# Queries, keys and values of paired token tiles by seven block products, with one half of x in SBUF

## The chip, the cores and the metric

The kernel runs on one core of a Trainium2 chip. Its engines are TensorE (PE, matmuls, with its weight loads shown apart as PEld), VectorE (DVE), ScalarE (ACT), GpSimd (POOL) and SyncE (SP, which here issues all DMA transfers). The metric is the device time of one execution in microseconds. The kernel before took 1124.25 us (median of 3 runs, 1122.22 to 1126.07).

## The reference

All is float32; S = 2048 tokens, D = 576 columns, H = 32 heads of 18 columns, F = 4608.

```python
xn = (x - mean) / sqrt(var + 1e-5)                 # over the 576 columns
q, k, v = split(xn @ wqkv)                         # 32 heads of 18
phi = lambda t: where(t > 0, t + 1, exp(t)) + 1e-6
pq, pk = phi(q), phi(k)
kv = einsum("bhsd,bhse->bhde", pk, v)              # one 18x18 state per head, over all tokens
z = einsum("bhsd->bhd", pk)
o = einsum("bhqd,bhde->bhqe", pq, kv) / (einsum("bhqd,bhd->bhq", pq, z) + 1e-6)
s = o @ wo
g = silu(gelu(xn @ w1 + b1) @ w2 + b2)
out = x + s * g
```

The state needs the keys and values of all tokens before the first query can be attended.

## The kernel before

**Numbers in two parts.** A float32 operand of a product is kept as h + l, two tiles of the faster type float32r: ACT copies the value into h (which rounds it), DVE or POOL subtracts h from the value to give l. A product is then hh + hl + lh, three matmuls for each 128 rows of the contraction. The 576 rows are four blocks of 128 and a rest of 64 rows; in the fifth block the upper 64 partitions hold the rest's l part, so it needs two matmuls. One tile's projection to 576 columns is 14 stationaries by two halves of 288 columns, 28 matmuls (`project`).

**Key/value stage.** It goes over 16 tiles of 128 tokens. For each: statistics and norm of x (`layernorm` on DVE with a power on POOL, `normalize_x` on ACT), five PE transposes into PSUM (`transpose_x`), h and l of the transposed x out of PSUM into `xh` and `xl`; 28 matmuls into `pk`; the feature map out of PSUM (`phi`, L226 to L229: exponential on ACT, two operations on DVE); 28 matmuls into `pv`, copied by ACT; ten small matmuls that add the tile to the state (`state`); POOL adds the keys to `zacc` (L441). Beside this, 27 operands for the feed-forward part's W2 are prepared: a sum on POOL (L288), h on ACT (L296), l on DVE (L301), and a store. All 16 tiles of x stay in SBUF as h and l, four blocks of 512 tokens.

**Query stage.** For each tile: 28 matmuls for the query, the feature map, the division by the denominator (POOL, DVE, POOL), five transposes, 28 matmuls with the folded state and Wo, and a store. Before the second tile Wo is folded into the state (`fold_wo`). Beside this, `XSums` makes four sums of blocks of x (s1 to s4) and one of the rests for each half of the tokens, from h and l in turns, 1024 columns at a time on DVE (L337), and splits them (L340, L341); one half is stored for later.

**Feed-forward part.** It goes over 18 steps, nine for each half of the tokens. Its products already use a seven-product scheme: two block rows, two block columns and two halves of the contraction, seven block products in the order 1, 6, 7, 5, 2, 3, 4 (`Up`, matmuls at L819), with DVE adding the results in that order. After the first nine steps the other half's x and sums are loaded from DRAM (L1115).

**Order.** Within the first two stages `in_order` fixes every engine, SP too, to the order in which the code is written. In the feed-forward part tables of step numbers set it. PSUM has three pairs of banks (`bank2`), used in turn by everything that takes a pair, and two single banks (`bank1`), which the state holds in the key/value stage.

## Time and profile before

| what | value |
|---|---|
| median of the runs | 1124.25 us |
| runs | 1122.22, 1124.25, 1126.07 us |
| span of the profiled execution | 1122.4 us |
| mean granted PE clock | 0.995 |
| DMA | 246.71 MB, 220 GB/s in the mean |
| HBM | 151.62 MB read, 92.47 MB written |

The profiled execution has no time of its own beside its span; its span lies 1.85 us below the median of the runs. Rows of groups read: line, engine, operation, output and inputs with shapes, count, busy us, mean ns of one, then the engine's idle time just before them and what ended it. Rows of windows read: from and to, length, busy us (and instructions) of PE, weight loads, DVE, ACT and POOL, the granted clock, the busy share of the DMA engines, GB/s. Rows of a timeline or of the chain read: start, us, engine, line, operation. Records of PE and DVE that follow each other overlap a little, so a mean is a latency and a pace is read from starts.

### The profile page before, as it was taken

Reading aid. Unit: us, or ns where it says so; the run is one execution under the profiler, and the core shown is the slowest. Engines: PE = TensorE matmul, PEld = TensorE weight load, DVE = VectorE, ACT = ScalarE, POOL = GpSimd, SP = SyncE. Lnnn points to the kernel's source line nnn. Section 1 sums busy time; section 2 is a strip of 40 time slices with the busy share of each in tenths; the row PEclk is TensorE's granted clock in tenths of the full one; section 3 lists DMA queues with packets and bytes.
Section 4 is the critical chain, followed back from the end, with each engine's and each line's share of the span. In section 5 each row is a group of like instructions: output and inputs, shape, how many; then the busy total and the mean of one; then the engine's idle time right before and its main releaser. Section 6 shows DMA issues by size and latency. Waiting matters only on the chain.

```text
span 1122.4 us, 18619 instructions
## 1 busy us (share of the span) xinstructions
PE 1108.1 (99%) x7008; PEld 1026.8 (91%) x7008; DVE 811.9 (72%) x1185; ACT 456.8 (41%) x801; POOL 443.0 (39%) x368
## 2 busy tenths in 40 slices
PE   8999998999999999999999999999999999999997
PEld 8999988999998989989889899898898998989987
DVE  6666658787687888878879888666475674764766
ACT  4444443233544454543544544524233242242352
POOL 4556533333353552535525434324233232242340
PEclk9999998999999999999999999999999999999999
DMA  7588631044659468475594769977766666756252
GB/s 295 193 335 301 222 124 41 33 172 160 228 224 342 170 241 301 160 290 206 205 340 172 262 244 389 368 254 258 221 208 212 214 204 211 231 197 222 84 170 88
DMA packets 83367, 246.71 MB, mean 220 GB/s; under 512 B 9229, under 2 KB 19981, under 8 KB 79695
## 3 DMA queue, kind: packets, MB, share of 16 engines
q1 hardware_dynamic: 83279, 245.54, 61.9%
q8 instruction: 55, 0.90, 0.3%
q14 instruction: 33, 0.27, 0.1%
HBM read 151.62 MB, written 92.47 MB: 217 GB/s over the span
## 4 chain that ended last, share of the span: by engine, by line
PE 95%; DVE 3%; DMA 0%; POOL 0%; ACT 0%; issue 0%; SPq 0%; DVEq 0%; ACTq 0%; POOLq 0%
PE pm L950 34%; PE e L819 12%; PE a L819 10%; PE zy L819 10%; PE pv L219 5%; PE pk L219 5%; PE b L819 4%; PE ps_s L592 4%; PE pq L219 4%; PE pd L1074 2%; PE ps_kva L256 1%; PE pt L196 1%; DVE xt L337 1%; PE ps_kw L518 1%; PE ptp L574 0%; DMA w<-wqkv 0%
## 5 line engine op out<-in xcount | busy, mean ns | idle before, releaser
L957 DVE TENSOR_TENSOR macc<-pm,macc 128x576 f32<-128x576 f32 x218 | 164.2, 753 | 56.9 <-PE pm L950 56.3
L616 ACT CAST h_h<-g 128x512 fp32r<-128x512 f32 x204 | 120.9, 621 | 139.8 <-PE pm L950 138.7
L619 DVE TENSOR_TENSOR h_l<-g,h_h 128x512 fp32r<-128x512 f32 x204 | 172.3, 844 | 0.0
L918 POOL TENSOR_TENSOR mid<-g 128x512 f32<-128x512 f32 x34 | 44.1, 1296 | 187.7 <-ACT g L827 187.7
L827 ACT ACTIVATE g<-b,b1c 128x512 f32<-128x512 f32 x36 | 24.8, 688 | 121.8 <-DVE b L845 121.7
L836 ACT COPY mid<-a 128x512 f32<-128x512 f32 x36 | 21.1, 585 | 109.3 <-PE a L819 109.3
L819 PE MATMUL a<-h0r,wa 128*128 128x512 f32 x180 | 58.6, 390 | 0.0
L819 PE MATMUL a<-xh,wa 128*128 128x512 f32 x180 | 58.5, 390 | 0.0
L839 DVE TENSOR_TENSOR mid<-b,mid 128x512 f32<-128x512 f32 x36 | 24.8, 689 | 46.5 <-PE b L819 35.4
L915 POOL TENSOR_TENSOR g<-g 128x512 f32<-128x512 f32 x34 | 52.4, 1542 | 13.1 <-DVE h_l L619 11.8
L912 POOL TENSOR_TENSOR g<-g 128x512 f32<-128x512 f32 x34 | 49.5, 1456 | 17.9 <-DVE h_l L619 16.6
L1044 POOL TENSOR_TENSOR fin1l<-fin1h,fin1l 128x288 f32<-128x288 f32 x8 | 6.4, 805 | 121.4 <-DMA fin1l<-s_dram 45.1
L819 PE MATMUL zy<-xh,w 128*128 128x512 f32 x144 | 50.2, 389 | 0.0
L819 PE MATMUL zy<-h1r,w 128*128 128x512 f32 x144 | 50.2, 389 | 0.0
L641 POOL TENSOR_TENSOR w1t<-w1raw 128x256 f32<-128x256 f32 x18 | 17.6, 977 | 81.4 <-DVE w L619 81.4
L909 POOL TENSOR_TENSOR g<-g 128x512 f32<-128x512 f32 x34 | 47.7, 1402 | 2.7
L852 DVE TENSOR_TENSOR e<-e,mid 128x512 f32<-128x512 f32 x36 | 25.1, 697 | 27.1 <-PE e L819 27.0
L555 POOL TENSOR_TENSOR pbuf<-phiq,den 128x576 f32<-128x576 f32 x16 | 20.9, 1305 | 57.8 <-DVE den L554 52.9
L827 ACT ACTIVATE g<-e,b1c 128x512 f32<-128x512 f32 x36 | 24.8, 689 | 43.0 <-DVE e L852 43.0
L288 POOL TENSOR_TENSOR w2r<-w2r 128x576 f32<-128x576 f32 x27 | 41.1, 1528 | 0.7
L819 PEld LDWEIGHTS a<-xh,wa 128*128 128x128 f32 x180 | 33.8, 188 | 6.8
L819 PEld LDWEIGHTS a<-h0r,wa 128*128 128x128 f32 x180 | 33.8, 188 | 6.8
(814 smaller groups left out, 3544.8 us busy)
## 6 DMA issues: line engine op xcount, KB each, us to landing
op<-w SPq DMA_DIRECT2D x72, 256.0 KB
w<-op SPq DMA_DIRECT2D x72, 256.0 KB
op<-w2o SPq DMA_DIRECT2D x27, 576.0 KB
w2raw<-w SPq DMA_DIRECT2D x10, 1152.0 KB
w1raw<-w SPq DMA_DIRECT2D x18, 640.0 KB
op_a<-wa SPq DMA_DIRECT2D x18, 640.0 KB
wa<-op_a SPq DMA_DIRECT2D x18, 640.0 KB
w2r<-w SPq DMA_DIRECT2D x9, 1152.0 KB
```

The costliest lines, as they stand in the source:

```text
L219: nc.tensor.matmul(ps[:, h, :HD], st, w[:, k, h * HD : (h + 1) * HD], start=(i == 0), stop=(i == len(seq) - 1),)
L592: nc.tensor.matmul(ps[:, h, :HD], st[:, k, :], w[:, k, h * HD : (h + 1) * HD], start=(i == 0), stop=(i == len(seq) - 1),)
L616: nc.scalar.copy(pair[0], src)
L619: eng.tensor_tensor(pair[1], src, pair[0].bitcast(F32), op=SUB)
L819: nc.tensor.matmul(ps, st, mv, start=first and n == 0, stop=n == len(seq) - 1, skip_group_check=True,)
L827: nc.scalar.activation(g, ps, AF.Gelu_apprx_tanh, bias=b1c[:, f : f + 1])
L909: tt(src[5, pr], A(1, 0), A(1, 1), op=ADD)
L912: tt(src[6, pr], src[5, pr], A(0, 0), op=SUB)
L915: tt(src[3, pr], A(0, 1), src[6, pr], op=SUB)
L918: tt(src[7, pr], A(0, 0), A(1, 0), op=SUB)
L950: nc.tensor.matmul(ps[:, q, :HD], hs[p][st][:, cs], m[:, p, :], start=(n == 0 and i not in CHAIN), stop=(n == len(seq) - 1), skip_group_ch ...
L957: nc.vector.tensor_tensor(dst, src, dst, op=ADD)
```

## The change

The seven-product scheme of the feed-forward part is applied to the projections. Two token tiles, one from each quarter of a half's tokens, form a pair (`pair_tile`), and there are eight pairs. `Proj` does both tiles' projection to 576 columns: seven products of six matmuls, four of which also take two matmuls of the rest, 50 in all. DVE makes five additions out of PSUM per pair and projection, ACT two copies. Pair 0's keys and values still go by the plain `project`, 28 matmuls a tile, since the sums aren't there yet.

For that, the weights are kept with their sums (`Weight`: seven h and seven l operands of 2 x 288 columns, and the rest); one tile, `wkq`, holds Wk and later Wq. The sums of x are made in the key/value stage from each pair's transposes: ACT copies the transposed tile to float32 in SBUF (`xf`), POOL makes the five sums (`x_sum`), ACT and DVE split them (`s_hi`, `s_lo`), and x's own split (`x_hi`, `x_lo`) now reads SBUF. `XSums` is gone from the query stage. The feature map also works in SBUF, on the finished keys (`phi_exp`, `phi_max`).

Only one half of x and its sums stays in SBUF (`xH`, `xL`, `xSH`, `xSL`). Each pair is stored to DRAM (`x_store`). The pairs 0 to 3 (second half of the tokens) come first, the pairs 4 to 7 overwrite their columns; the queries start with pairs 4 to 7 and pairs 0 to 3 are loaded back one by one (`x_reload`). After nine feed-forward steps the other half is loaded with four transfers (`x_swap`). A table of steps, 14 to a pair, says after which product each piece of this work is issued (`plan_pair`). W2's sums stand there too, three to a pair for pairs 2 to 6, and the other twelve in the query stage.

On DVE, one tile of the key/value stage reads so before (`xl` and `xh` splits, two W2 splits, statistics, feature map):

```order
L205 TENSOR_TENSOR xl_89<-pt_541,xh_88 128x4x128
L206 TENSOR_TENSOR xh_88<-pt_541,xh_88 64x128
L301 TENSOR_TENSOR w2o_550<-w2r_304,w2o_550 128x576
L301 TENSOR_TENSOR w2o_552<-w2r_306,w2o_552 128x576
L168 BN_STATS st_556<-x_405 128x6
L169 BN_STATS st_556<-x_405 128x6
L171 BN_AGGR mv_559<-st_556 128x2
L172 TENSOR_SCALAR mv_559<-mv_559 128x1
L180 SCALAR_TENSOR_TENSOR mv_559<-mv_559 128x1
L227 TENSOR_SCALAR ek_565<-ek_565 128x576
L229 SCALAR_TENSOR_TENSOR phik_568<-pk_512,ek_565 128x576
```

And now, on DVE, from the feature map of pair 2's keys through the first products of its values (`ab` and `ze` are PSUM, `mu` the running sums, `scr` the float32 copies of x and s):

```order
L387 TENSOR_SCALAR e_151<-e_151 128x576
L388 SCALAR_TENSOR_TENSOR k_147<-k_147,e_151 128x576
L343 TENSOR_TENSOR mu_143<-ab_807,mu_142 128x288
L387 TENSOR_SCALAR e_152<-e_152 128x576
L388 SCALAR_TENSOR_TENSOR k_148<-k_148,e_152 128x576
L346 TENSOR_TENSOR mu_144<-ze_808,mu_143 128x288
L349 TENSOR_TENSOR v_150<-ze_808,mu_144 128x288
L295 TENSOR_TENSOR xSL<-scr,xSH 128x8x128
L299 TENSOR_TENSOR xSH<-scr,xSH 64x128
L355 TENSOR_TENSOR v_149<-ze_808,mu_143 128x288
```

The additions that free PSUM (L343 to L355) stand between the feature map and x's and s's splits, and those read SBUF alone.

On POOL, two tiles read so before (power, W2 sums, sum of the keys):

```order
L173 TENSOR_TENSOR mv_454<-mv_454,nhalf 128x1
L288 TENSOR_TENSOR w2r_304<-w2r_304 128x2x288
L288 TENSOR_TENSOR w2r_306<-w2r_306 128x2x288
L441 TENSOR_TENSOR zacc<-zacc,phik_463 128x576
L173 TENSOR_TENSOR mv_559<-mv_559,nhalf 128x1
L288 TENSOR_TENSOR w2r_306<-w2r_306 128x2x288 x2
L441 TENSOR_TENSOR zacc<-zacc,phik_568 128x576
```

And now, on POOL, one pair, which has five sums of x more:

```order
L235 TENSOR_TENSOR mv_915<-mv_915,nhalf 128x1
L436 TENSOR_TENSOR w2r_687<-w2r_687 128x2x288 x2
L288 TENSOR_TENSOR scr<-scr 128x256 x4
L288 TENSOR_TENSOR scr<-scr 128x128
L235 TENSOR_TENSOR mv_1013<-mv_1013,nhalf 128x1
L436 TENSOR_TENSOR w2r_687<-w2r_687 128x2x288
L554 TENSOR_TENSOR zacc<-zacc,k_147 128x576
L554 TENSOR_TENSOR zacc<-zacc,k_148 128x576
```

One W2 sum less and five sums of x more stand in the same span of tokens.

On ACT, the opening reads so before, from the V weight's casts to the third tile (`pt` is a transposed tile in PSUM, `pk` keys in PSUM):

```order
L243 CAST wv_h<-raw_v 128x576 x4
L243 CAST wv_h<-raw_v_143 128x576
L204 CAST xh_86<-pt_246 128x5x128
L226 ACTIVATE ek_264<-pk_207 128x576
L434 COPY v_298<-pv_269 128x576
L191 ACTIVATE xn_262<-x_193,mv_258 128x576
```

And now, on ACT (`pp` is a plain projection in PSUM, `xn_269` the third tile's norm, `e_151` the exponential of the first tile's keys):

```order
L471 COPY rt<-pt_246 128x640
L479 CAST xSH<-pt_246 128x2x128
L266 CAST xH<-rt 128x3x128
L146 CAST wv_h<-raw_195 128x2x288 x2
L248 ACTIVATE xn_269<-x_202,mv_265 128x576
L248 ACTIVATE xn_269<-x_202,mv_265 128x64
L391 ACTIVATE e_151<-pp_217 128x576
L146 CAST wv_h<-raw_195 128x2x288 x2
L157 CAST wv_rh<-rr_196 128x576
L518 COPY scr<-pt_311 128x640
L264 CAST xH<-scr 128x5x128
```

The first exponential of keys moved behind the third tile's norm, and three of the V weight's casts behind it.

The diff, cut to what the prediction speaks of:

```diff
+    xH = xp.tile([P, 8, 512], F32R, tag="xH", name="xH")
+    xL = xp.tile([P, 6, 512], F32R, tag="xL", name="xL")
+    xSH = xp.tile([P, 9, 512], F32R, tag="xSH", name="xSH")
+    xSL = xp.tile([P, 8, 512], F32R, tag="xSL", name="xSL")
...
+    def x_lo(p, s, src=None):
+        cs, src = pair_cols(p), xf(p, s) if src is None else src
+        tt = nc.vector.tensor_tensor
+        if s == 0:
+            tt(xL[:, 0:4, cs], src[:, :4], xH[:, 0:4, cs].bitcast(F32), op=SUB)
+        else:
+            tt(xL[:, 4:6, cs], src[:, 2:4], xH[:, 5:7, cs].bitcast(F32), op=SUB)
+        r = xH[64:, 4 + 3 * s, cs]
+        tt(r, src[64:, 4], r.bitcast(F32), op=SUB)
...
+    def x_sum(p, i, eng):
+        a, b = xf(p, 0), xf(p, 1)
+        s1, s2, s3, s4 = (s_raw[:, k : k + 2] for k in (0, 2, 4, 6))
+        out, u, v, op = {
+            1: (s1, b[:, 0:2], b[:, 2:4], ADD), 2: (s2, s1, a[:, 0:2], SUB),
+            3: (s3, a[:, 0:2], b[:, 0:2], SUB), 4: (s4, a[:, 2:4], s2, SUB),
+            5: (s_raw[:, 8], a[:, 4], b[:, 4], SUB),
+        }[i]
+        eng.tensor_tensor(out, u, v, op=op)
+    def s_lo(p):
+        cs = pair_cols(p)
         nc.vector.tensor_tensor(
+            xSL[:, :, cs], s_raw[:, :8], xSH[:, :8, cs].bitcast(F32), op=SUB
         )
...
+    def x_store(p):
+        cs = pair_cols(p)
+        for t, a, b in X_PARTS:
+            nc.sync.dma_start(x_dram[p // 4][:, a:b, cs], t[:, :, cs].bitcast(F32))
...
+        def step(self, i):
+            A, B, Z, E = self.A, self.B, self.Z, self.E
+            tt = nc.vector.tensor_tensor
+            a, b = self.dst
+            if i == 1:
+                self.mm(A, 1)
+                nc.scalar.copy(self.m1, A)
+            elif i == 6:
+                self.mm(B, 6)
+                tt(self.u1, B, self.m1, op=ADD)
+            elif i == 7:
+                self.mm(Z, 7)
+                tt(self.u2, Z, self.u1, op=ADD)
+            elif i == 5:
+                self.mm(E, 5, (1, 1))
+                tt(b[:, HD:], E, self.u2, op=ADD)
+            elif i == 2:
+                self.mm(A, 2, (0, 0), first=False)
+                nc.scalar.copy(a[:, :HD], A)
+            elif i == 3:
+                self.mm(E, 3, (1, 2), first=False)
+                tt(a[:, HD:], E, self.u1, op=ADD)
+            else:
+                self.mm(Z, 4, (0, 1))
+                tt(b[:, :HD], Z, self.u2, op=ADD)
...
+    def phi_max(r, e):
+        nc.vector.tensor_scalar(e, e, 1.0, 1e-6, op0=ALU.min, op1=ADD)
+        nc.vector.scalar_tensor_tensor(r, r, 1.000001, e, op0=ADD, op1=ALU.max)
...
+        if 1 <= p and p + 1 < NPAIR and p + 1 >= 2:
+            q = p + 1
+            add(base + 2, transpose_to_xf, q, 1)
+            add(base + 3, x_hi, q, 1)
+            add(base + 4, x_lo, q, 1)
+            for i, at in {1: 3, 2: 3, 3: 4, 4: 4, 5: 5}.items():
+                add(base + at, x_sum, q, i, GP)
+            add(base + 8, s_hi, q)
+            add(base + 10, s_lo, q)
+            add(base + 11, x_store, q)
...
-                for k, at in {"h0": 13, "l0": 13, "s2": 13, "h1": 15, "l1": 15, "s1": 15, "s4": 15}.items():
-                    add(base + at, load_x_part, k)
+                for k, at in ((0, 13), (1, 13), (2, 15), (3, 15)):
+                    add(base + at, x_swap, k)
```

822 lines of the change are left out of this document (426 added, 396 removed), and 4 rows, old and new, of the table SUMS.

## The prediction

> **What bounds the kernel now.** I read the page first: busy times and the shares of the chain of waits.
>
> ```profile
> PE 1108.1 (99%) x7008; PEld 1026.8 (91%) x7008; DVE 811.9 (72%) x1185; ACT 456.8 (41%) x801; POOL 443.0 (39%) x368
> ...
> PE 95%; DVE 3%; DMA 0%; POOL 0%; ACT 0%; issue 0%; SPq 0%; DVEq 0%; ACTq 0%; POOLq 0%
> ```
>
> TensorE (PE) is busy for the whole span and is 95% of the chain, so at first sight fewer matmuls mean less time. Next the windows by stage: busy us and instructions of PE, weight loads, DVE, ACT and POOL, the granted clock, the DMA share.
>
> ```profile
> 13.60:153.00 139.40, 139.32 (x1091) 139.02 (x1090) 92.58 (x166) 62.84 (x104) 75.74 (x67) 1.00 0.68 254
> 153.00:298.20 145.20, 141.05 (x1016) 136.01 (x1015) 110.33 (x163) 52.57 (x99) 49.96 (x39) 0.96 0.32 112
> 298.20:1122.40 824.20, 818.21 (x4849) 743.19 (x4847) 600.64 (x838) 333.35 (x587) 309.89 (x249) 1.00 0.66 231
> ```
>
> The first window is the key/value stage, the second the query/attention stage, the third the feed-forward part, which the change hardly touches. In the first, DVE works 92.58 of 139.40 us and POOL 75.74; in the second PE is idle at least 145.20 - 141.05 = 4.15 us. The chain in order of time gives PE's pieces:
>
> ```profile
> 26.81 3.74 PE pk L219 x28
> 30.55 0.55 PE pt L196 x5
> 31.09 0.88 PE ps_kva L256 x8
> 31.97 0.13 PE ps_kvb L256 x2
> ...
> 321.17 22.43 PE pm L950 x168
> ```
>
> A projection of one tile is 28 matmuls in 3.74 to 3.77 us; the five transposes take 0.55, the state sums 0.88 + 0.13. A token tile costs 3.77 + 3.74 + 0.55 + 1.01 = 9.07 us, a pair 18.1. The last row has 288-column matmuls with a new stationary each time, as the changed projections have: 22.43 / 168 = 0.1335 us.
>
> **What the change takes away on PE.** A pair's projection goes from 56 to 50 matmuls, and 22 of 24 pair-projections change: 132 matmuls, 132 x 0.1335 = 17.6 us. That would be the gain if PE stayed the bound. A pair of the key/value stage would take 100 x 0.1335 + 2 x 0.55 + 2 x 1.01 = 16.5 us instead of 18.1.
>
> **What it puts on DVE and POOL there.** The rows that price this, first of the key/value stage, then of the next:
>
> ```profile
> L180 DVE SCALAR_TENSOR_TENSOR mv<-mv 128x1 f32<-128x1 f32 x13 | 17.9, 1375 | 9.4 <-POOL mv L173 9.4
> L229 DVE SCALAR_TENSOR_TENSOR phik<-pk,ek 128x576 f32<-128x576 f32 x14 | 10.6, 758 | 0.5
> L205 DVE TENSOR_TENSOR xl<-pt,xh 128x512 fp32r<-128x512 f32 x14 | 9.7, 691 | 31.3 <-ACT xh L204 31.3
> L227 DVE TENSOR_SCALAR ek<-ek 128x576 f32<-128x576 f32 x14 | 6.3, 447 | 0.0
> L168 DVE BATCH_NORM_STATS2 st<-x 128x6 f32<-128x288 f32 x13 | 5.9, 453 | 0.0
> L171 DVE BATCH_NORM_AGGREGATE mv<-st 128x2 f32<-128x12 f32 x13 | 2.7, 209 | 0.4
> L206 DVE TENSOR_TENSOR xh<-pt,xh 64x128 fp32r<-64x128 f32 x14 | 4.1, 294 | 0.2
> ```
>
> ```profile
> L525 DVE TENSOR_TENSOR kw_l<-ps_kw,kw_h 128x288 fp32r<-128x288 f32 x2 | 0.9, 457 | 3.8 <-ACT kw_h L524 3.8
> L244 DVE TENSOR_TENSOR kw_l<-kw,kw_h 128x576 fp32r<-128x576 f32 x1 | 0.7, 695 | 0.0
> L337 DVE TENSOR_TENSOR xt<-xt,xh 128x1024 f32<-128x1024 f32 x2 | 2.4, 1218 | 0.0
> ```
>
> ```profile
> L441 POOL TENSOR_TENSOR zacc<-zacc,phik 128x576 f32<-128x576 f32 x14 | 19.8, 1411 | 2.6 <-DVE phik L229 2.6
> L173 POOL TENSOR_TENSOR mv<-mv,nhalf 128x1 f32<-128x1 f32 x13 | 7.1, 549 | 49.1 <-DVE mv L172 49.1
> ```
>
> A middle pair (2 to 5) has on DVE: ten additions out of PSUM, 10 x 0.457 = 4.6, and the statistics of two tiles, 2 x (2 x 0.453 + 0.21 + a one-column add, taken as 0.2) = 2.6. These 7.2 us read at most one operand from SBUF. The others read two, or run in the fast one-input form of L227: three W2 splits 3 x 0.695, x's splits 0.69 + 0.41 + 1.22 + 3 x 0.29, the feature map 2 x (0.447 + 0.695), two one-column products at 0.2 or less, together 8.0. DVE has 15.2 us in all. POOL has five 576-wide operations at 1.41, four 256-wide sums at 0.73 (row below), one of 128 (estimated 0.5), two powers at 0.55: 11.6.
>
> The 8.0 and the 11.6 exclude each other. L180 works on one column and takes 1375 ns when POOL has just begun a W2 sum, and here, in the feed-forward part, operations with two SBUF inputs lengthen on both engines (mean alone 1296 ns on POOL, 0.67 us on DVE):
>
> ```profile
> L918 POOL TENSOR_TENSOR mid<-g 128x512 f32<-128x512 f32 x34 | 44.1, 1296 | 187.7 <-ACT g L827 187.7
> ```
>
> ```profile
> 325.92 1.62 POOL L912 TENSOR_TENSOR g<-g 128x512 f32<-128x512 f32 x1
> 327.62 1.62 POOL L915 TENSOR_TENSOR g<-g 128x512 f32<-128x512 f32 x1
> 331.63 0.73 POOL L646 TENSOR_TENSOR w1raw<-w1raw 128x256 f32<-128x256 f32 x1
> ```
>
> ```profile
> 326.98 1.11 DVE L619 TENSOR_TENSOR h_l<-g,h_h 128x512 fp32r<-128x512 f32 x1
> 328.68 1.11 DVE L619 TENSOR_TENSOR h_l<-g,h_h 128x512 fp32r<-128x512 f32 x1
> 335.43 0.67 DVE L619 TENSOR_TENSOR h_l<-g,h_h 128x512 fp32r<-128x512 f32 x1
> 341.12 0.41 DVE L619 TENSOR_TENSOR w<-w1t,w 128x256 fp32r<-128x256 f32 x1
> ```
>
> POOL's ends are 327.62 + 1.62 - 325.92 - 1.62 = 1.70 us apart, each round holding one POOL and one DVE operation. L205, with one input in PSUM, stays at 691 ns in the mean, as long as L619 alone, though POOL is at work in that stage. So a middle pair needs 8.0 + 11.6 = 19.6 us by full records, or 19.6 x 1.70 / (1.30 + 0.67) = 16.9 by that stretch. Between them lie the chains: the feature map is four such operations in a row, among POOL's third W2 sum and first `zacc` sum, and the addition of product 5 of the values is queued behind it on DVE, before PE may write product 3 into the same bank. I take 19.6, since DVE also waits there for products and for ACT. The ends are 16.5 (PE's own) and 23.
>
> The Trainium skill ("SBUF — State Buffer", section "SBUF: two separate sides") says that the pair of ports shared by the two engines is locked for the whole instruction and the loser blocks. By that the 19.6 stands; by the 1.70 us of this trace part of each record overlaps, the four middle pairs would give 4 x 2.7 = 11 us back, and the sum would be 1144 instead of 1155.
>
> ACT's part, four casts and two copies of x and s, two norms, two exponentials, four copies of 288 columns and three W2 casts, is near 11 us of the 19.6, so I cost it at nothing there. So too the stores of x, 2.03 MB a pair: with W2's stores and loads 5.6 MB in 19.6 us, 284 GB/s, where the first window moved 254 at a DMA share of 0.68. If they aren't hidden, the next x tiles, behind them on SP, come late, and DVE's statistics with them. In pair 1 that is so: the first tile of pair 3 loads behind the first store.
>
> Before, two token tiles cost 18.1, so the middle pairs lose 4 x 1.5. Pair 1 also carries the splits of the V weight's sums and a second split of s: DVE 15.2 - 2.1 + 2 x 1.3 + 1.5 = 17.2, of which 10.0 exclude POOL; POOL four 576-wide weight sums in place of three W2 sums, 13.0; 23.0, plus some 4 us that DVE is late at its start: 27 (22 to 30). Pair 6 lacks the loads ahead, 17. Pair 7 rewrites the weight tile to Wq, five splits on ACT and DVE between the feature map and the additions: 19. Pairs 1 to 7: 27 + 78.4 + 36 = 141.4 against 153.0 - 26.8 = 126.2: **+15.2**, with 114 (-12) and 163 (+37) as ends.
>
> **The opening.** Pair 0 is still projected plainly, two tiles for K, then for V, and everything for pair 1 must be ready behind it. Rows:
>
> ```profile
> 12.85 0.77 PE L196 MATMUL pt<-ident,xn 128*128 128x128 f32 x5 [0.61 <-DVE xn L177]
> 19.60 1.20 ACT L191 ACTIVATE xn<-x,mv 128x576 f32<-128x576 f32 x2 [1.46 <-DVE mv L180]
> ```
>
> ```profile
> L226 ACT ACTIVATE ek<-pk 128x576 f32<-128x576 f32 x15 | 9.8, 654 | 1.4 <-issue 1.4
> L204 ACT CAST xh<-pt 128x640 fp32r<-128x640 f32 x13 | 9.0, 692 | 18.3 <-PE pt L196 18.3
> L296 ACT CAST w2o<-w2r 128x576 fp32r<-128x576 f32 x27 | 16.9, 676 | 0.0
> ```
>
> Up to the second tile's normalized x nothing changes (its transposes at 12.85). Then, step by step: transposes to 13.9; ACT copies it, 0.69, and casts K's part for the plain projection, 0.4, so PE begins tile 1 near 15.1 and ends near 19.0. Its next transposes need the third PSUM pair, which holds tile 0's keys until their feature map is made. That is behind, on ACT, a cast (0.5), two weight casts (2 x 0.68) and the third tile's norm (1.20), which waits for DVE's split and statistics (0.7 + 1.3), POOL's split (1.41) and power (0.55): norm ends at 20.3, exponential 0.65, DVE 0.45 + 0.76: 22.1. The fourth tile repeats it: transposes 22.7; ACT has three weight casts left of which the last ends at 22.9; copy and cast to 24.3; splits, statistics, power, norm to 29.0; exponential; one POOL sum to wait for; feature map 31.6; transposes 32.2. Then pair 1's sums: copy and cast 33.5; DVE splits and two sums, with POOL between, 36.0; a weight split of 1152 columns (about 1.3) 37.3; POOL 0.73 + 0.5; ACT's cast of s (about 1.2) 39.8; DVE's split 1.5; the fifth tile's statistics, power, product, 43.2; norm 44.4; transposes 45.0. PE's work in this stretch is four projections and four transposes, and it is idle for the rest. Before, the same point (two tiles projected) stands at 26.81. **+18.2**; without any POOL wait about +13, with one more operation in each round +22.
>
> **Clock.** In the query stage a PE wait of 1.69 us is followed by slower matmuls (below), and that window's granted clock is 0.96 where the key/value stage has 1.00:
>
> ```profile
> 183.52 0.74 PE L574 MATMUL ptp<-ident,pbuf 128*128 128x128 f32 x5 [1.69 <-DVE phiq L229]
> ...
> 185.30 0.64 PE L592 MATMUL ps_s<-kw_h,th 128*128 128x288 f32 x2
> ```
>
> Waits of 2 to 4 us inside each pair could do the same, some 3 us of slow PE each time, mostly hidden while DVE is the bound. I add **+2**, between 0 and 8. The Trainium skill ("TensorE: Matmul & The Clock Gate", "What's actually happening") has the clock halved only after about 3.4 us of idleness; by it the term would be nearly 0, by the row above it can come sooner.
>
> **The query stage.** Eight pairs at 50 instead of 56 matmuls: 48 x 0.1335 = 6.4 less. x's sums, 20 operations of 1024 columns, and their splits leave DVE, so the waits of the second window go down from 4.15 or more; four rounds get W2 splits before the addition that frees product 3's bank. Net 1 better: **-7.5** (-11 to -3). The reloads of x (2 MB a round) stand on SP ahead of Wo's row shifts, and the DMA share of that window is 0.32, so they fit.
>
> **The feed-forward part.** The reload of the other half's x, 31 x 512 x 128 x 4 bytes = 8.1 MB, comes where DMA is full:
>
> ```profile
> L1115 SPq DMA_DIRECT2D l0r<-x_dram x1: 319/319/319, 680.0 to 680.0; - x1
> ```
>
> ```profile
> L1115 SPq DMA_DIRECT2D s4r<-x_dram x1: 320/320/320, 694.4 to 694.4; - x1
> ```
>
> ```profile
> 684.50:708.30 23.80, 23.80 (x176) 23.53 (x175) 19.81 (x28) 9.22 (x14) 7.96 (x6) 1.00 1.01 415
> ```
>
> Before, its first three parts are issued from 680.0, during the last products. Now each of the four tiles is read until product 3 or 4, so all start near 684.5, 4.5 us later, and the sums that landed last must be there for product 6 instead of product 3. At 415 GB/s a full delay is up to 6 us; how much slack there was no row shows: **+2.5** (0 to 6).
>
> **Sum.** 18.2 + 15.2 + 2 - 7.5 + 2.5 = +30.4; span 1122.4 + 30.4 = 1152.8. The profiled span lies 1.85 below the median of the runs, 1124.25, which I keep: **1155 us**. Under 0.3% (3.4 us) a difference can't be told here.
>
> **Rivals.**
> - *PE stays the bound* (0.10): DVE and POOL fit beside 16.5 us per pair. For it: PE is never idle in 27 to 153 us and POOL's records overlap. Against: 15.2 us of DVE work of 16.5. Pairs 114 (-12), query -7.5, reload 0, opening +8: 1124.25 - 11.8 = 1112. It decides the sign if the pairs run at 16.5 and the opening loses under 17.
> - *The exchange is cheaper* (0.22): the 1.70 us rows hold and the chains cost little. Against it: nothing but the orders, in which the same waits come back each pair. Middle pairs 17.3, pair 1 22, the last two 33, opening +14: 14 - 2 - 7.5 + 1 = +5.5, 1130 (1121 to 1140).
> - *Waits and slow clock feed each other* (0.20): for it the 183.52 row, against it that PE has 3 us to spare per pair. PE stops before product 3 of the values, resumes at half pace, DVE then waits for it: middle pairs 23, pair 1 30, last two 41, opening +20: 20 + 36.8 - 4 + 4 = +57, 1181.
> - The change not doing what it says: the instruction order has 132 matmuls fewer, so this is left out.
>
> **Numbers.** My forecast (1140 to 1170) has 0.46; the rest, 0.02, is a stall that I don't see. To hold 8 in 10 the range goes from 1126 to 1182: it leaves out the first rival, the low end of the second and the high end of the third. Faster 0.09, within 0.3% 0.06, slower 0.85.
>
> **What would show it.** The first seven-product matmul at about 45 us; middle pairs 19 to 21 us apart with PE idle before product 3, released by DVE; DVE's L388 and L295 longer than 0.7 and 1.2 us where POOL runs; the first feed-forward matmul near 326 us instead of 298. I am wrong if DVE is idle between products in the middle pairs, or the opening ends before 35.

## The result, and the profile after

The changed kernel took 1256.8 us (median of 4 runs, 1255.4 to 1258.2) against 1124.05 us for the kernel before: a ratio of 1.118, with a 95% interval from 1.117 to 1.120. The forecast was 1155 us, between 1126 and 1182. The direction was right and the size was four times too small.

The profiled span is 1255.0 us. First the page of the changed kernel, engines and the chain that ended last:

```profile
PE 1136.6 (91%) x6876; PEld 1037.4 (83%) x6876; DVE 851.7 (68%) x1283; ACT 480.7 (38%) x850; POOL 494.2 (39%) x419
...
PE 76%; DVE 9%; DMA 7%; ACT 3%; issue 2%; SPq 1%; POOL 1%; DVEq 0%; POOLq 0%; ACTq 0%
```

PE has the 132 matmuls less, and still records 28 us more busy time; in the first two windows below the granted clock is 0.91, so its matmuls take longer there. Its share of the chain fell from 95% to 76%, so it now waits, for DVE, DMA and ACT. Next the windows by stage (busy us of PE, weight loads, DVE, ACT, POOL; granted clock, DMA share, GB/s): pairs 1 to 7, the query stage, the feed-forward part. The first begins with the first seven-product matmul, the second with the first for queries.

```profile
46.38:242.83 196.45, 137.50 (x897) 127.47 (x896) 119.56 (x213) 70.65 (x119) 93.56 (x90) 0.91 0.55 180
242.83:428.85 186.02, 150.96 (x979) 139.88 (x978) 103.58 (x180) 56.81 (x114) 66.51 (x51) 0.91 0.48 161
428.85:1255.00 826.15, 818.59 (x4849) 743.10 (x4847) 601.83 (x838) 333.33 (x587) 310.18 (x249) 1.00 0.66 231
```

No engine fills the first two windows: in the pairs PE is busy for 137.5 of 196.5 us, DVE for 119.6, POOL for 93.6. That is a picture of engines waiting for each other, and not of one that is full. Against the stages of the kernel before:

| stage | before | after | difference | forecast |
|---|---|---|---|---|
| opening, to the first seven-product matmul (before: to the third tile's keys) | 26.8 | 46.4 | +19.6 | +18.2 |
| pairs 1 to 7 | 126.2 | 196.5 | +70.3 | +15.2, and +2 for the clock |
| query stage | 145.2 | 186.0 | +40.8 | -7.5 |
| feed-forward part | 824.2 | 826.2 | +2.0 | +2.5 |
| sum | 1122.4 | 1255.0 | +132.6 | +30.4 |

The middle pairs 2 to 5 are 27.45 us each (82.70 to 192.50 for four), where 19.6 were forecast; pair 1 is 36.3 (forecast 27), pair 6 22.6 (17), pair 7 27.7 (19).

**One middle pair.** The timeline of PE shows where it stands; the last bracket is the idle time before the matmul and what ended it. In time, these are product 6 and product 4 of the keys, product 6 and product 5 of the values:

```profile
139.18 0.40 PE L329 MATMUL ab<-wkq_h,xSH 128*128 128x288 f32 x1 [0.49 <-ACT mu L340]
148.81 0.40 PE L329 MATMUL ze<-wkq_h,xH 128*128 128x288 f32 x1 [1.69 <-DVE k L355]
151.54 0.40 PE L329 MATMUL ab<-wv_h,xSH 128*128 128x288 f32 x1 [0.60 <-ACT mu L340]
157.97 0.61 PE L329 MATMUL ze<-wv_h,xSH 128*128 128x288 f32 x1 [4.57 <-DVE mu L346]
```

None of these four waits is for data, or for a bank that is still read. Product 5 writes bank E, and L346 reads bank Z. Product 4 writes Z, and L355 reads E. Product 6 writes B, and ACT's copy L340 reads A. Each time it is the other bank of the same two-bank PSUM tile. The instruction list of PE, which is the program with its waits before it runs, has these waits too (the last two matmuls of the values' product 7 in a middle pair, then the first two of product 5):

```
L329 MATMUL ze_1236<-wv_l,xSH 128x288
L329 MATMUL ze_1236<-wv_h,xSL 128x288
L329 MATMUL ze_1236<-wv_h,xSH 128x288 [waits DVE_49]
L329 MATMUL ze_1236<-wv_l,xSH 128x288
```

The third row is the first matmul of product 5. Its bank was free, and yet it waits for DVE.

DVE and POOL at the same place in pair 2, the feature map of the second tile's keys on DVE and then L346 (the second fence is POOL):

```profile
99.35 1.28 DVE L387 TENSOR_SCALAR e<-e 128x576 f32<-128x576 f32 x1
100.67 1.83 DVE L388 SCALAR_TENSOR_TENSOR k<-k,e 128x576 f32<-128x576 f32 x1
102.43 0.45 DVE L346 TENSOR_TENSOR mu<-ze,mu 128x288 f32<-128x288 f32 x1
```

```profile
98.65 1.67 POOL L436 TENSOR_TENSOR w2r<-w2r 128x576 f32<-128x576 f32 x1
100.28 1.61 POOL L554 TENSOR_TENSOR zacc<-zacc,k 128x576 f32<-128x576 f32 x1
```

L387 takes 0.45 us and L388 0.76 when POOL is quiet (run e8 below). Here L387 ends at 100.63, 0.31 us after POOL's first sum, and L388 at 102.50, 0.61 us after POOL's second: with the times that they take alone, both did their work when POOL's instruction was all but over. L346 is queued behind them, and PE behind L346.

**One query round.** The chain in order of time, in the second of the four rounds that carry W2 work:

```profile
305.92 8.30 DMA w2r<-w
314.26 0.09 issue
314.35 1.44 POOL w2r L436
315.81 0.68 ACT w2o L440
...
317.79 0.46 DVE rt L349
318.29 2.30 PE ze L329 x8
```

A chunk of W2 lands 8.3 us after its issue, which stands behind the reload of x in SP's list; POOL sums it, ACT casts it, DVE splits it (the row left out), and only then DVE comes to L349, for which product 3 waits. The four rounds take 28.8, 23.8, 24.0 and 20.1 us, the next one without W2 work 18.1.

**The feed-forward part** waits for the second half of x once, as forecast (waits of PE, total, times, longest):

```profile
PE b L954 <- DMA xSL<-x_dram: 1.7, 1, 1.7
```

### The profile page after: what moved, and what is told of

The parts are those of the page before. It is cut to its first block, busy times and chain, and to the rows that moved or that the text cites. A ratio compares the mean times of both kernels' runs of the same rounds, so it can differ in the third digit from the quotient of the medians.

```text
span 1255.0 us, 18591 instructions
## 1 busy us (share of the span) xinstructions
PE 1136.6 (91%) x6876; PEld 1037.4 (83%) x6876; DVE 851.7 (68%) x1283; ACT 480.7 (38%) x850; POOL 494.2 (39%) x419
## 4 chain that ended last, share of the span: by engine, by line
PE 76%; DVE 9%; DMA 7%; ACT 3%; issue 2%; SPq 1%; POOL 1%; DVEq 0%; POOLq 0%; ACTq 0%
PE pm L1085 29%; PE e L954 11%; PE zy L954 9%; PE a L954 9%; PE ze L329 5%; PE b L954 4%; PE ps_s L769 4%; DMA w2r<-w 3%; PE ab L329 2%; DMA xSL<-x_dram 2%; PE pd L1204 2%; ACT xn L248 1%; DVE w2o L445 1%; DMA kr<-kw 1%; DVE e L387 1%
## 5 line engine op out<-in xcount | busy, mean ns | idle before, releaser
L954 PE MATMUL a<-xH,wa 128*128 128x512 f32 x360 | 117.1, 390 | 0.0
L954 PEld LDWEIGHTS a<-xH,wa 128*128 128x128 f32 x360 | 67.6, 188 | 13.6
L962 ACT ACTIVATE g<-b,b1c 128x512 f32<-128x512 f32 x36 | 24.8, 689 | 122.0 <-DVE b L980 122.0
L954 PE MATMUL e<-xSH,wb 128*128 128x512 f32 x216 | 67.6, 394 | 0.0
L974 DVE TENSOR_TENSOR mid<-b,mid 128x512 f32<-128x512 f32 x36 | 24.8, 690 | 47.5 <-PE b L954 36.4
L1047 POOL TENSOR_TENSOR g<-g 128x512 f32<-128x512 f32 x34 | 49.6, 1459 | 18.2 <-DVE h_l L796 16.9
L954 PE MATMUL a<-xL,wa 128*128 128x512 f32 x144 | 56.2, 390 | 0.0
L329 PE MATMUL ze<-wkq_h,xSH 128*128 128x288 f32 x90 | 30.8, 342 | 23.1 <-DVE scr L346 12.1
L954 PEld LDWEIGHTS e<-xSH,wb 128*128 128x128 f32 x216 | 40.5, 188 | 12.1 <-DVE b L980 3.8
L954 PE MATMUL b<-xSH,w 128*128 128x512 f32 x144 | 50.2, 389 | 0.0
L954 PE MATMUL zy<-xSH,w 128*128 128x512 f32 x144 | 50.2, 389 | 0.0
L954 PE MATMUL zy<-xH,w 128*128 128x512 f32 x144 | 50.2, 389 | 0.0
L954 PE MATMUL e<-xSH,w 128*128 128x512 f32 x144 | 50.2, 389 | 0.0
```

The costliest lines, as they stand in the source:

```text
L329: nc.tensor.matmul(ps, st, mv, start=first and n == 0, stop=n == len(seq) - 1, skip_group_check=True,)
L954: nc.tensor.matmul(ps, st, mv, start=first and n == 0, stop=n == len(seq) - 1, skip_group_check=True,)
L1047: tt(src[6, pr], src[5, pr], A(0, 0), op=SUB)
```

## The experiments

All eleven start from the changed kernel; beside them the kernel before took 1123.6 to 1124.7 us. e10 is a median of 4 runs, the others are one run each; the four runs of the changed kernel lie 2.8 us apart, so a difference of 3 us between two runs says nothing by itself. "Pair" is the mean of pairs 2 to 5, from one first matmul of product 1 to the next; "query stage" runs from the first query matmul to the first of the feed-forward part.

| run | edit | time | pair | query stage |
|---|---|---|---|---|
| | changed kernel | 1256.8 | 27.5 | 186.0 |
| e1 | other pairing of PSUM banks | 1215.2 | 23.2 | 172.4 |
| e2 | reloads of x behind the W2 loads | 1242.8 | 27.4 | 173.3 |
| e3 | pairs without W2 work | 1245.3 | 24.7 | 187.8 |
| e4 | PE kept busy in two waits | 1254.0 | 26.3 | 188.0 |
| e5 | e1 and e2 | 1208.8 | 23.3 | 165.4 |
| e6 | e5, lists in another order | 1196.7 | 21.6 | 160.3 |
| e7 | query rounds without W2 work | 1238.1 | 27.4 | 168.6 |
| e8 | e1, POOL quiet in the pairs | 1187.6 | 17.6 | 172.0 |
| e9 | old pairing, POOL quiet in the pairs | 1233.0 | 21.8 | 187.9 |
| e10 | e6, lists ordered further | 1192.4 | 20.7 | 161.8 |
| e11 | e10, query rounds without W2 work | 1182.6 | 20.8 | 151.6 |

### e1: which banks share a tile

```diff
-            self.A, self.B = ab[:, 0, :HD], ab[:, 1, :HD]
-            self.Z, self.E = ze[:, 0, :HD], ze[:, 1, :HD]
...
+            self.A, self.Z = az[:, 0, :HD], az[:, 1, :HD]
+            self.B, self.E = be[:, 0, :HD], be[:, 1, :HD]
```

(The lines left out take the two tiles in alternating order from one projection to the next. The pairing and this order were not tried apart.)

> The edit: the seven products' four PSUM banks are paired as A with Z and B with E, in place of A with B and Z with E, and the order in which the two pairs are taken alternates, so that the tile product 1 needs is the one read earlier. Nothing else changes. In the trace of the changed kernel PE stands before product 5 until DVE's second addition, L346, is done (4.6 us in each middle pair), which reads Z while product 5 writes E; before product 4 until L355, which reads E while product 4 writes Z (1.7 and 0.5 us); before product 6 until ACT's copy of A (0.5 us, 13.8 us over the program). Theory 'a wait holds for the whole PSUM tile': these waits are for the other bank of the same tile, and they go or shrink to what the other pairing leaves. Middle pairs 27.5 down to 21 to 23 us, the 6.3 us before product 6 of pair 1 down to under 1, the late query rounds unchanged near 18: total 1205 to 1220 us. Rival 'DVE's list sets the pace': PE would only wait at another product, since DVE still does the two feature maps of the keys before L346: middle pairs 26 to 27.5, total 1243 to 1255.

Measured: 1215.2 us, pairs of 24.0, 22.5, 22.9 and 23.3, the query stage 13.6 us shorter. In the same 54 us of time the waits of PE were (total, times, longest), first in the changed kernel, then here:

```profile
PE ze L329 <- DVE mu L346: 9.1, 2, 4.6
PE ze L329 <- DVE k L355: 3.4, 2, 1.7
PE ab L329 <- ACT mu L340: 2.2, 4, 0.6
PE ze L329 <- DVE v L355: 1.1, 2, 0.6
```

```profile
PE be L335 <- DVE mu L349: 5.2, 3, 1.9
PE az L335 <- ACT mu L346: 5.2, 3, 1.7
PE az L335 <- DVE mu L352: 0.3, 1, 0.3
```

(The same additions are L343, L346 and so on in the one, six lines further down in the other: L349 is the old L343, which reads B, beside E.) The waits behind the second addition and behind L355 are gone; what is left are the waits that this pairing has, again for the other bank of the tile: product 5, which writes E, waits for L349, which reads B, and product 7, which writes Z, for ACT's L346, which copies A. Not one operation differs, so the wait for the whole tile is shown. What this pairing and order save of it is 41.5 us of span, and some of it is left. Theory "DVE's list sets the pace" falls. The first theory's total holds and its mean pair is 0.2 us over its range; but the 6.3 us in pair 1 became 3.3 us before product 7, where under 1 was expected.

### e2: the reload of x behind the W2 load

```diff
-            if r < NPAIR // 2:
-                x_reload(Q_ORDER[r + 4])
             if 1 <= r <= 4:
                 w2_load(r + 4, w2rp, "w2raw")
...
             if r == 0:
                 fold_wo()
+            if r < NPAIR // 2:
+                x_reload(Q_ORDER[r + 4])
```

> The edit: in the query rounds the four reloads of x stand behind the load of a W2 chunk on SP, and in the first round behind the fold of Wo with its row shifts; the K/V stage is untouched. Theory 'the reload stands in the way': in the changed kernel the chain has 11.0 us for the row shifts kr, issued behind 2 MB of reloads, and three rounds of 24 us with 4.4 us of reload issues on SP and then 8.3 to 8.7 us for a W2 chunk of 1.18 MB. With the chunk first, it starts 4.4 us sooner and has the queues to itself, 4 to 5 us: rounds of 24 become 16 to 18, row shifts 4 to 5; query stage 20 to 30 us shorter, total 1225 to 1235. Rival 'one W2 buffer': the load can't start before the round's last split has read the buffer, and the first sum of the next round needs it, so a round can't be shorter than load plus sum plus cast whatever stands before it: only the 4.4 us of issues go, rounds of 19.5 to 21, total 1240 to 1246.

Measured: 1242.8 us; rounds of 20.1. The W2 load no longer ends the wait; the chain of a round is now

```profile
305.90 1.16 POOL pbuf L733
307.06 1.41 POOL w2r L436
308.49 0.68 ACT w2o L440
...
310.94 1.52 DVE w2o L445
312.88 1.32 PE ze L329 x8
```

So the place of the reload cost 4 us in each of three rounds (the fourth took 20.1 us before), and the rest of the chain, sum, cast and split ahead of the addition, stays. The wait for the row shifts in the first rounds didn't get shorter (11.0 us, then 11.7): it was not made by the reload ahead of them. The rival's ranges for the total and for the rounds hold, but not by its reason: the load, which it put at the head of each round, is no longer on the chain.

### e3: pairs without W2 work

```diff
-                add(base + a, w2_sum, 3 * c + j)
-                add(base + b, w2_hi, 3 * c + j)
-                add(base + d, w2_lo, 3 * c + j)
+                add(base + d, w2_put, 3 * c + j)
```

(`w2_put` stores the raw block in both places of the operand.)

> The edit: in pairs 2 to 6 the three W2 sums on POOL, the casts on ACT and the splits on DVE are left out, and the raw blocks are stored in their place with the same bytes, so the first five chunks of W2 hold raw values and not the operands. What is left out in a pair is POOL 4.5, ACT 2.0 and DVE 2.6 us, and the DVE time that the splits wait (1.8 us before the second, for ACT). Theory 'exclusive port', as predicted: DVE's and POOL's two-input operations can't overlap, so the pairs shorten by the sum of both, 4.5 + 2.6 = 7 us, to 20 or 21: total 1215 to 1222. Theory 'waits of the whole PSUM tile, and the half clock behind them': only the waits on ACT and the lengthened L388 (1.83 for 0.76) go, 3 us a pair, to 24 or 25: total 1237 to 1243.

Measured: 1245.3 us, pairs of 24.7. Taking 4.5 us of POOL and 2.6 us of DVE work from a pair gave 2.8 us. The sum of the two engines' exclusive work does not set the pair; the second theory's range for the pair holds, and the total lies 2 us above its range.

### e4: PE kept busy

```diff
...
+            for _ in range(n):
+                nc.tensor.matmul(
+                    ps_kv[1][:, 128:416], xH[:, 0, self.cs], self.w.op(1)[0][:, 0],
+                    start=False, stop=False, skip_group_check=True,
+                )
```

(n is 32 ahead of the values' product 5 and 12 ahead of the keys' product 4, in pairs 1 to 6.)

> The edit: matmuls of no use (288 columns, into columns of the state's second bank that nothing reads) are put on PE ahead of product 5 of the values (32) and of product 4 of the keys (12) in pairs 1 to 6, so that PE doesn't idle there; 32 at 0.1335 us are 4.3 of the 4.6 us that it waited. The result's values are unchanged. Theory 'half clock': behind each of these waits the next products ran at half pace (eight matmuls in 2.29 us instead of 1.07, five transposes in 1.07 instead of 0.55), and DVE then waited for them (2.4 us before L349): with PE kept busy the pairs lose 1.8 to 2.5 us each, total 1240 to 1244. Rival 'DVE has slack behind the wait': the pairs keep 27 to 27.5 us, total 1251 to 1256.

Measured: 1254.0 us, pairs of 26.3. The values' product 5 starts when the second addition ends (L346, here L357), as in the changed kernel, and runs at full pace:

```profile
126.53 0.38 DVE mu L357
126.95 1.33 PE ze L330 x8
128.28 0.55 PE pt L258 x5
```

Eight matmuls in 1.33 us for 2.29, five transposes in 0.55 for 1.07; but the pair gains only 1.15 us, less than the first theory's 1.8 and more than the rival's 0.5. Most of the pair's length is there without the half pace. The span is 2.7 us shorter, which one run can't tell from nothing: pairs 1 to 5 gained 6.1 us, pair 6 lost 2.0, and the query stage, which the edit leaves alone, came out 2.0 longer. The total lies in the range of the rival "DVE has slack".

### e5: both edits together

The edit is the two diffs of e1 and e2.

> The edit: the new pairing of PSUM banks (A with Z, B with E) and the later reloads of x together. Apart, the first took 41 us from the span (29 in the K/V pairs, 13.6 in the query stage) and the second 14, all in the query stage. If they remove different waits there, they add up: 1255 - 41 - 14, 1199 to 1204 us. If the rounds of 24 us are one chain, from a chunk's landing through sum, cast and split to the addition that frees product 3's or 4's bank, each takes out part of the same chain: 1207 to 1214.

Measured: 1208.8 us. Apart the edits took 41.5 and 13.9 us from the span, together 47.9 (in the query stage 13.6 and 12.7 apart, 20.6 together): in the query rounds they take out parts of the same chain, from the chunk to the addition that product 3 or 4 waits for. The second reading holds.

### e6: the lists in another order

```diff
-        add(base + 8, phi_max, k_t[1], e_t[1])
+        add(base + 9, phi_max, k_t[1], e_t[1])
...
-            for j, (a, b, d) in enumerate(((0, 3, 3), (2, 5, 5), (6, 9, 13))):
+            for j, (a, b, d) in enumerate(((0, 3, 4), (2, 4, 6), (6, 9, 13))):
...
-                    add(base + 2 * j, w2_sum, n)
-                    add(base + 2 * j + 1, w2_hi, n)
-                    add(base + 2 * j + 2, w2_lo, n)
+                    add(base + j, w2_sum, n)
+                    add(base + (2, 4, 5)[j], w2_hi, n)
+                    add(base + (3, 5, 6)[j], w2_lo, n)
```

> The edit: on top of the new bank pairing and the later reloads, the lists are put in another order. K/V pairs: the second feature map of the keys stands behind the addition of product 7 of the values (L346 in the changed kernel) instead of ahead of it; the first two W2 splits on DVE one step later, so that DVE doesn't wait for ACT's cast. Query rounds: each split of W2 behind an addition instead of ahead of it. No operation is added or taken away. Theory 'the lists' order costs, not the engines' capacity': with the same work the middle pairs, 22.8 us with the new pairing, go to 19 to 20.5, the rounds of W2 to 17 to 18: 20 to 28 us less than the run with pairing and reloads alone, 1175 to 1184. Theory 'exclusive port' as predicted: DVE's two-input operations and POOL's need 19.6 us a pair only if they never wait, so the order brings at most 1 us a pair: 5 to 10 us less.

Measured: 1196.7 us, 12.1 us less than e5, pairs of 21.6, W2 rounds of 17.6 to 23.8. That is between the two theories, nearer to the second: the order is worth something, but with all the work in place the pairs don't come to 20.

### e7: query rounds without W2 work

```diff
-                    add(base + 2 * j, w2_sum, n)
-                    add(base + 2 * j + 1, w2_hi, n)
-                    add(base + 2 * j + 2, w2_lo, n)
+                    add(base + 2 * j + 2, w2_put, n)
```

> The edit, against the changed kernel: in the query rounds the W2 chunks are loaded and stored as before, but not summed, cast and split (POOL, ACT, DVE); so four chunks of W2 hold raw values and not the operands. The reloads stand where they were. Theory 'a chain from the load through the W2 work': in the rounds of 24 us product 3 waits for an addition that is queued on DVE behind a split, that for a cast, that for a sum, that for the load. Without this work rounds 2 to 5 take what the later ones take, 18 us: 4 x 6 = 24 us less, total 1228 to 1234. Rival 'the transfers': the reloads and chunks themselves hold the round, 22 us or more: total 1246 to 1252.

Measured: 1238.1 us; the two rounds that took 24 us now take 18.1, with the reloads and loads in their old places:

```profile
303.66:321.72 18.06, 15.90 (x119) 15.20 (x118) 10.20 (x19) 5.04 (x11) 5.31 (x5) 1.00 0.95 307
```

(Window of one round; busy PE, weight loads, DVE, ACT, POOL, clock, DMA share, GB/s.) So the transfers themselves don't hold a round; the chain through sum, cast and split does. The span is 18.6 us shorter where 24 were expected: the round ahead of them went from 28.8 only to 24.8, held by the row shifts, and the one behind them from 20.1 to 18.4.

### e8 and e9: a quiet POOL, with the new pairing and with the old

```diff
-        add(base + 9, k_sum, k_t[0])
-        add(base + 11, k_sum, k_t[1])
```

(and the edit of e3; e8 has that of e1 too)

> The edit: on top of the new bank pairing the W2 sums, casts and splits of pairs 2 to 6 (raw blocks stored instead) and the sums of the keys' feature map on POOL (so the denominator is only 1e-6) are left out. In a middle pair POOL keeps five small sums of x and two powers, 4.6 us instead of 12.7; DVE loses 2.6 us of splits. Theory 'exclusive port': with POOL quiet, L387 and L388 go back from 1.23 and 1.85 us to 0.45 and 0.76, and the middle pairs, 22.8 us with the pairing alone, go to PE's own 16.5 to 17.5: spans 27 to 32 us under that run, 1182 to 1187 total. Theory 'the lists still wait for each other': L388 shortens all the same, but the pairs stay at 19.5 to 21: 1197 to 1205.

> The edit: the changed kernel with its own pairing of PSUM banks, and with POOL quiet in the pairs: W2's sums, casts and splits of pairs 2 to 6 left out (raw blocks stored), the sums of the keys' feature map on POOL left out (so the denominator is only 1e-6). It is the fourth corner beside the changed kernel (middle pairs 27.5 us), the new pairing (24.0, 22.5, 22.9, 23.3) and both (17.6). Theory 'exclusive port alone', as predicted: without POOL's work DVE has slack and the pairs fall to 17 to 19 whatever the pairing: 1255 - 4 x 9 - 10, total 1205 to 1212. Theory 'waits of the whole PSUM tile first': PE still stands before products 6, 5 and 4 for an addition that reads the other bank and is behind the feature maps in DVE's list; only the lengthening goes (L387 1.22 to 0.45, L388 1.83 to 0.76) beside what leaving W2 out gave: 22 to 23.5: total 1230 to 1238.

Measured: 1187.6 us with pairs of 17.6, and 1233.0 us with pairs of 21.8. The two groups of DVE's feature map, from 110 to 160 us (count, busy, mean ns), first with the new pairing alone, then with POOL quiet:

```profile
L394 DVE SCALAR_TENSOR_TENSOR k<-k,e 128x576 f32<-128x576 f32 x4 | 5.2, 1306 | 0.1
L393 DVE TENSOR_SCALAR e<-e 128x576 f32<-128x576 f32 x4 | 3.5, 875 | 0.0
```

```profile
L394 DVE SCALAR_TENSOR_TENSOR k<-k,e 128x576 f32<-128x576 f32 x6 | 4.6, 760 | 0.2
L393 DVE TENSOR_SCALAR e<-e 128x576 f32<-128x576 f32 x6 | 2.7, 450 | 0.0
```

The four corners of the pair's time are 27.5 (as changed), 23.2 (new pairing), 21.8 (quiet POOL) and 17.6 (both). The two edits nearly add up: 4.3 and 5.7 us apart, 9.8 together. With both a pair is 1.1 us above PE's own 16.5. So "waits of the whole PSUM tile first" holds for e9 (its pair 0.2 us under the range), and for e8 "exclusive port" is 0.1 us off for the pair and 0.6 for the total.

The 5.7 us are not all POOL's hold on DVE. The W2 work gave 2.8 (e3), with DVE's and ACT's part of it left out too. The two sums of the keys on POOL, which take 1.41 us each and nothing of DVE's or ACT's time, gave the other 2.9 (e9 against e3). Here is the second L387 of pair 4 in e3, and the start of the values' products 5 and 4 in that pair, first in e3, then in e9:

```profile
146.66 1.57 DVE L387 TENSOR_SCALAR e<-e 128x576 f32<-128x576 f32 x1
149.45 0.40 PE L329 MATMUL ze<-wv_h,xSH 128*128 128x288 f32 x1 [2.74 <-DVE mu L346]
155.56 0.40 PE L329 MATMUL ze<-wv_h,xH 128*128 128x288 f32 x1 [0.55 <-DVE v L355]
```

```profile
140.72 0.40 PE L329 MATMUL ze<-wv_h,xSH 128*128 128x288 f32 x1 [1.61 <-DVE mu L346]
145.27 0.40 PE L329 MATMUL ze<-wv_h,xH 128*128 128x288 f32 x1 [0.55 <-DVE v L355]
```

L387 takes 1.57 us in e3, where it starts just after a sum of the keys (POOL at 146.52), and 0.45 in e9. These 1.1 us are in PE's wait, 2.74 against 1.61. The other 1.6 us are PE's own: behind the longer wait its matmuls fell to 0.24 us apart (from 150.5 to 153.7), behind the shorter one they stayed at 0.13, so products 5 to 4 start 6.11 us apart in the one and 4.55 in the other. POOL's hold costs twice here, once on DVE and once through PE's clock.

### e10 and e11: ordered further, and the floor of the query stage

e10 starts from e6. It takes the first feature map behind the values' product 6 too (the second already stood behind product 7), lets x's splits read the transposes in PSUM, and puts the splits of the folded Wo behind the additions of the second round. The diff is cut; the second tile's statistics, the keys' sums and one W2 split also move by one to three steps.

```diff
-        add(base + 7, phi_max, k_t[0], e_t[0])
+        add(base + 8, phi_max, k_t[0], e_t[0])
...
-            add(base + 12, x_lo, p + 2, 0)
+            add(base + 12, lo_ps, p + 2, 0)
...
-                    add(base + 2 * k, split_kw, k, nc.vector)
+                    add(base + 6, split_kw, k, nc.vector)
```

(`lo_ps` is `x_lo` with the transposes in PSUM as its source.) e11 adds the edit of e7.

> The edit: on top of the new bank pairing, the later reloads and the re-ordered lists, further orders: both feature maps of the keys stand behind the addition of product 6 of the values, and their sums on POOL a step later; the second tile's statistics in the same place; in the first query rounds the splits of the folded Wo behind the additions; x's splits in the pairs read the transposes in PSUM in place of the copy in SBUF (one SBUF input instead of two). Same operations in all. Theory 'the lists' order and the port': pairs from 21.2 to 22.4 down to 19 to 20, and 5 to 8 us less between the folded Wo and the second round: 1175 to 1182 us. Theory 'exclusive port only': the sum of DVE's and POOL's two-input work, 19.6 by the prediction less 2.5 us for x's splits, isn't the limit yet, and the pairs stay at 21 or more: 1188 to 1195. Neither comes near the kernel before, since the opening's 20 us and PE's 15.2 us of a query round at 18 stay.

> The edit: the previous best lists, with the W2 work of the query rounds left out (loaded and stored raw, neither summed, cast nor split, so four chunks of W2 hold raw values). It asks whether the query stage could give the 7.5 us that were predicted, once its waits are gone. PE's own work in a round is 50 x 0.1335 for the products, 2 x 3.72 for the attention and 2 x 0.55 for transposes, 15.2 us. Theory 'only the W2 chain was in the way': rounds of 15.3 to 16.5 from the third on, the stage 135 to 142 us against 145.2 before and 161.8 in the best lists: total 1166 to 1172. Theory 'the additions between the products still set the round': 17 us, as the last two rounds already show (21.1 and 17.0 in the best lists): stage 144 to 152, total 1174 to 1183.

e10 measured 1192.4 us (1190.5 to 1193.4), a ratio of 1.060 to the kernel before, interval 1.059 to 1.062; pairs of 20.7, so the second theory's total holds, while the pair lies between the two theories. Which of the moves shortened the pair was not tried apart. The re-ordered query rounds gained nothing over e6: the third cast of a round now waits for the store of the first operand, since two tiles take turns, and the row shifts stay. The chain:

```profile
222.80 10.27 DMA kr<-kw
...
266.39 4.75 DMA op<-w2o
271.24 0.68 ACT w2o L446
```

e11 measured 1182.6 us. Its W2-less rounds take 16.7 us, and its query stage 151.6 us is still 6.4 above the kernel before. From 215 to 356 us PE waits in the main for the first addition (L349), and once for DVE, whose list stands behind the row shifts:

```profile
PE be L335 <- DVE scr L349: 9.4, 7, 1.8
PE be L335 <- DVE th L773: 6.7, 1, 6.7
PE ps_kw L714 <- ACT kw L718: 0.6, 1, 0.6
```

The rounds lie between the two theories' values; the second theory's ranges for the stage and the total hold. No version came near the kernel before: the opening's 20 us and the pairs' 20.7 for 18.1 remain.

## Why the prediction was right or wrong

**Opening: right in size, in part by luck.** First seven-product matmul at 46.4 us, forecast 45. Two errors ahead of the fourth tile's transposes cancelled. The prediction had the norm end at 29.0 and the transposes end at 32.2, behind the second feature map. The norm began at 30.46 and ended at 31.66; and the transposes didn't wait for the feature map, which ended later, at 34.44:

```profile
31.38 1.28 PE L258 MATMUL pt<-ident,xn 128*128 128x128 f32 x5 [2.21 <-ACT xn L248]
33.68 0.76 DVE L393 SCALAR_TENSOR_TENSOR k<-pp,e 128x576 f32<-128x576 f32 x1
```

From there on each step came within 2 us of the forecast. But product 6 behind it waited 6.3 us for ACT's copy of A, behind a norm in ACT's list; that was counted nowhere, and is the whole-tile wait once more.

**Pairs: the step that failed.** It was "So a middle pair needs 8.0 + 11.6 = 19.6 us by full records", taken as the pair's time, with the words that PE waits "before PE may write product 3 into the same bank". In the pairs no wait before product 3 is recorded at all. The long wait stood two products earlier, before product 5, and shorter ones before 4 and 6, for the other bank of the tile. They weren't in the sum, though PE's instruction list shows them. What the other pairing takes away of them is 4.3 us a pair (e1), and 4.1 with POOL quiet (e8 against e9). ACT, "costed at nothing", also holds DVE: in pair 4 DVE stands 1.83 us before a W2 split (at 150.66) for ACT's cast.

The exclusion itself was right in kind: L387 and L388 lengthen beside POOL, and with POOL quiet the pair loses 5.7 us, of which PE's half pace is a part. But the sum was not the pair's time. Leaving out 4.5 us of POOL's work and 2.6 of DVE's gave 2.8 (e3). With the other pairing and re-ordered lists, all work in place, the pair comes to 21.6 (e6), 2.0 above the 19.6. The 20.7 of e10 can't be set beside the 19.6: x's splits read PSUM there, which by the prediction's own prices takes 0.69 + 0.41 + 2 x 0.29 = 1.7 us out of the sum. So no run with all the work in place came below the sum, and none came near it: I used what was at best a lower bound as a forecast. In lists with a fixed order, each operation waits behind all others of its engine. That DVE would be idle between products in the middle pairs was named as what would prove me wrong, and it was idle: 2.4 us before L349, waiting for product 5. As to the rule that the loser of the shared ports blocks for the whole instruction (the Trainium skill, "SBUF — State Buffer", section "SBUF: two separate sides"): the rows of L387 and L388 beside POOL's agree, and the overlap of 1.70 us that I set against it doesn't apply there.

**Clock: not settled in size.** +2 was forecast. Keeping PE busy in its two longest waits gave 2.7 us of span, which is not clear of noise; it gave 6.1 us in pairs 1 to 5 (e4), so the term was too small. That it would be "mostly hidden while DVE is the bound" fits the 1.15 us a middle pair that came back, but DVE wasn't the bound, and without the W2 work the half pace costs 1.6 us a pair (e3 against e9). The rival "waits and slow clock feed each other" had the middle pairs nearest (23 us), but by a cause that e4 rules out: with the pace back at full, 26.3 of 27.5 us stay.

**Query stage: wrong in sign.** The step was "four rounds get W2 splits before the addition that frees product 3's bank. Net 1 better". The place was right; its price was taken as next to nothing, where the rounds went to 24 us. What was left out is what stands ahead of the split: a load into the only buffer, issued behind the reload of x, then a sum and a cast. Without the sums, casts and splits the stage is 17.4 us shorter (e7). "The reloads ... so they fit" is right for the bandwidth, though with little to spare (e7 moves 307 GB/s in rounds of 18 us, at a DMA share of 0.95), and wrong for the place on SP, worth 12.7 us of the stage (e2). The other pairing is worth 13.6 us there (e1), and these three overlap: 43.7 us apart, 34.4 in e11, which has all three edits and later orders. Its stage is 151.6 us, so even then the 7.5 us were not had. The row shifts of the folded Wo, 10.3 us, are on the chain there, and the round behind them takes 24.6 us where the later ones take 16.7; in the kernel before they are not on the chain of that stretch. That the missing time is this one wait is argued and not shown.

**Feed-forward part: right.** +2.0, forecast +2.5; PE waited once, 1.7 us, for the last of the four loads.

One sum of the rivals is off: seven pairs at 16.5 us are 115.5 us and not 114; it decides nothing.

Still open: pair 1 and pair 7 were 9 us longer than forecast each; of pair 7's, 6.4 went with the new pairing (21.3 us in e1), of pair 1's 5.2; the rest wasn't taken apart.

## What to carry to other kernels

Here the program's waits go by PSUM tiles and not by banks. Where that is so, products that follow each other should not write banks of one tile: read the waits in the instruction list, and ask of each whether it is for data. A sum of two engines' exclusive work is at best a lower bound and not a forecast; to forecast a period, follow it once through every engine's list, and price each place where an operation stands behind one that itself waits. A load that feeds a sum, a cast and a split ahead of a needed addition should, it seems, stand a whole round earlier, in a second buffer; no run here tried that.

## What was unexpected in the hardware

How long PE may wait before its pace falls isn't one number here. In the pairs and query rounds of the changed kernel waits of up to 1.74 us were followed by matmuls 0.13 us apart (but for three of 0.55 us right behind a longer one), and those from 3.4 us on by matmuls 0.2 to 0.24 us apart; between 1.9 and 3.1 us both were seen. In its opening a wait of 1.39 us (at 23.67), with one of 0.96 us two microseconds ahead, was followed by matmuls 0.24 us apart from 24.56 on. In e1 a wait of 1.92 us slowed PE where one of 1.66 us had ended 3 us earlier:

```profile
91.78 0.40 PE L335 MATMUL az<-wv_h,xSH 128*128 128x288 f32 x1 [1.66 <-ACT mu L346]
94.77 0.61 PE L335 MATMUL be<-wv_h,xSH 128*128 128x288 f32 x1 [1.92 <-DVE mu L349]
95.17 0.44 PE L335 MATMUL be<-wv_l,xSH 128*128 128x288 f32 x1
95.41 0.44 PE L335 MATMUL be<-wv_h,xSL 128*128 128x288 f32 x1
```

(Starts from 95.17 on are 0.24 us apart.) That fits short waits counting together; no run here tested it, and how they would be summed stays open. In the same way the slow pace of the kernel before, behind a wait of 1.69 us, isn't a rule: behind the wait of 1.69 us at 148.81 the matmuls came at 0.13.
